# Attention score tiles below the diagonal read back from their mirror tiles, MLP and attention steps alternating

## The chip, the cores and the metric

One core of one Trainium2 chip runs the whole program in one launch. The metric is device time in microseconds of that core, from runs of the same program on the same inputs; lower is better.

## What is computed

Three layers follow each other on 24576 tokens (8 sequences of 3072) of width 256:

```python
# attention, per sequence: u, v are 3072 x 256, z is 3072 x 64
scores = matmul(z, z.T) / 3072
x = u * matmul(maximum(scores, 0) ** 2, v)
# MLP: w_in 256 x 2048, w_out 2048 x 256
h = x @ w_in
x = (h * sigmoid(h)) @ w_out
# eight experts, one per token (argmax of x @ w_gate), 256 -> 1024 -> 256
h = maximum(x[mask] @ w1[e], 0)
out[mask] = gate[mask] * output_gate[mask, e] * (h @ w2[e])
```

The score matrix of a sequence is z times its own transpose, so it is symmetric: the score of query s and key t is that of query t and key s.

## The kernel before

**Numbers.** The matmuls run on fp32r operands. To keep fp32 accuracy each operand is split into a high part (`hi`, rounded to fp32r) and the rest (`lo` = value - `hi`), and a product is three matmuls: high by high, high by low, low by high.

**Blocks and steps.** Tokens are cut into 48 blocks of 512 (`NBLK`), 6 per sequence: block (b, q) is query block q of sequence b. Attention of a block has 24 steps (`KT`), one for each key tile of 128 keys. A step has a front and a back. The front (`att_items`, lines 203 to 228) makes a score tile of 128 keys by 512 queries in PSUM with two matmuls (lines 214 and 215; z has only 64 columns, so its high and low parts are stacked on the 128 partitions of `hl`), ScalarE takes Relu (line 217) and Square (line 219) into a buffer `t1`, then `hi` is cast (line 225, VectorE; line 223, ScalarE, in some early steps), and `lo` is a VectorE subtraction (line 227), which is issued at the next step. The back (lines 230 to 247) adds the tile's product with v to the accumulator: six matmuls of 512 columns (lines 240 to 242).

The MLP of a block has 16 steps (`NF1`) of 128 hidden columns: six matmuls in front (line 271), Sigmoid on ScalarE (line 273), product on VectorE (line 275), `hi` on ScalarE (line 278), `lo` on VectorE (line 280), and twelve matmuls of 256 columns in the back (lines 305 to 307). After attention of a block `finish` (line 253, two VectorE instructions) multiplies by u, and `split_x` (lines 195 and 197) makes the MLP's operands `xh` and `xl`.

**Order.** All steps stand in one list, `items`. The main loop (lines 836 to 849) issues at index i the tasks that are due, the front of step i, the `lo` of the step before, the back of step i-3 (`LOOK`), and then further tasks as long as a credit lasts that the finished step's budget fills up. From block 3 on, the list is: 7 attention steps of block n (`PRE`), all 16 MLP steps of block n-1, the other 17 attention steps of block n. Engines run their own instructions in this order, and semaphores come from the buffers: `ps` (PSUM, 4), `acc` (2), `t0` (2), `t1` (3), `hi` and `lo` (4 each), shared by attention and MLP steps.

**Tasks.** Loads of z and v go through SP's DMA queue into a ring of four staging buffers (`raw`, `DEPTH`) in the order of a list `stream`; each use of one (`f_prep`) stages the next. Line 163 loads z, line 180 v, line 209 u (two tiles of 256 KB per block, at step 4). Per sequence there are 6 key operands `hl` and 12 pairs `vh`, `vl` to be prepared, per block one `hh`, `ll`. Routing of a finished MLP block is 16 tasks of two VectorE dot products each (`dot`, line 315), a task `pick`, a task `rank` and four indirect DMAs to the scratch tensor `scr`. The experts (from about 4320 us) read gathered rows of `scr`; there, `m2_block` (line 527) already loads 512 x 32 blocks as 128-byte pieces, eight DMAs for two tiles, and `m2_trans` (line 581) turns them with VectorE's 32x32 transpose.

Of the kernel before, what the change touches and what calls it, by code (L numbers as in the profile page):

```python
# [9 lines left out]
F32 = mybir.dt.float32  # L10
# [31 lines left out]
def moe_chain(tc, zT, uT, vp, win, wout, w12, wgT, wogT, out):  # L42
# [19 lines left out]
    NBM = min(NB, (N - NA * TQ) // TB + E // 2)  # L62
    assert NBLK > 3 and KT > 2 * PRE and NF1 >= 16 and NA <= P and NB <= P and N // P <= 256
    ZS = 2.0 ** -10
    AS = (1.0 / (S * ZS)) ** 2

    with ExitStack() as ctx:
# [117 lines left out]
        def split_x(b, q, last=False):  # L185
# [10 lines left out]
            for c in range(ND):  # L196
                nc.vector.tensor_tensor(out=l[c], in0=x[c], in1=r32(h[c]), op=ALU.subtract)

        def att_items(b, q, hold):
            st = {}  # L200
            early = (b, q) < (0, 2)

            def front(k):
                def f():
                    if k == LOOK + 1:
                        st["u"] = []
                        for c in range(ND):
                            ut = mk(ap_, [P, TQ], F32, "u", 2)
                            nc.sync.dma_start(out=ut, in_=uT[b, q, :, c, :])
                            st["u"].append(ut)  # L210
                    h, l = qs[(b, q)]
                    ps = psum()
                    lhs = hl[k // NS][:, (k % NS) * P:(k % NS + 1) * P]
                    nc.tensor.matmul(ps, lhs, h, start=True, stop=False)  # L214
                    nc.tensor.matmul(ps, lhs, l, start=False, stop=True)  # L215
                    r = mk(cp, [P, TQ], F32, "t0", 2)
                    nc.scalar.activation(r, ps, AF.Relu)  # L217
                    a = mk(cp, [P, TQ], F32, "t1", 3)
                    nc.scalar.activation(a, r, AF.Square)  # L219
                    hi = mk(cp, [P, TQ], F32R, "hi", 4)  # L220
                    lo = mk(cp, [P, TQ], F32R, "lo", 4)
                    if early and q and k % 2:
                        nc.scalar.activation(hi, a, AF.Copy)
                    else:
                        nc.vector.tensor_copy(hi, a)  # L225
                    st[k] = (hi, lo)
                    return lambda: nc.vector.tensor_tensor(out=lo, in0=a, in1=r32(hi), op=ALU.subtract)  # L227
                return f

            def back(k):  # L230
                def f():
                    hi, lo = st.pop(k)
                    if k == 0:
                        st["acc"] = accum()
                    acc = st["acc"]
                    for c in range(ND):
                        o = k % 2 * D + c * P
                        h = vh[k // 2][:, o:o + P]
                        l = vl[k // 2][:, o:o + P]
                        nc.tensor.matmul(acc[:, c, :], h, hi, start=k == 0, stop=False)  # L240
                        nc.tensor.matmul(acc[:, c, :], h, lo, start=False, stop=False)  # L241
                        nc.tensor.matmul(acc[:, c, :], l, hi, start=False, stop=k == KT - 1)  # L242
                    if k == KT - 1:
                        later(2, 1.2, finish, 0)
# [9 lines left out]

            return [Item(front(k), back(k), EARLY if early else 0.7 if q == NQ - 1 else 0.5) for k in range(KT)]

# [194 lines left out]
        def final_tables():  # L451
# [19 lines left out]
            for e in range(E):  # L471
                later(4 + 2 * e, 0.0, pad(fr, e))

# [169 lines left out]
        order = [("a", 0, 0, KT), ("a", 1, 0, KT), ("a", 2, 0, PRE), ("m", 0, 0, NF1), ("a", 2, PRE, 2 * PRE), ("m", 1, 0, NF1), ("a", 2, 2 * PRE, KT)]  # L643
        for n in range(3, NBLK):
            end = NF1 - (PRE if n == NBLK - 1 else 0)
            order += [("a", n, 0, PRE), ("m", n - 1, 0, end), ("a", n, PRE, KT), ("m", n - 1, end, NF1)]
        order += [("m", NBLK - 1, 0, NF1)]
# [23 lines left out]

        def prep(due, rel, load, use):
            stream.append((due, rel, len(stream), load, use))

# [11 lines left out]
        for n, (b, q) in enumerate(blocks):  # L686
            if q == 0:
                for j in range(NHL):
                    rel = att_step(n - 1, (j + 1) * NS - 1) + 1 if n else 0
                    prep(max(att_step(n, j * NS) - (0 if n else 2), rel), rel, load_zz(b, j), f_hl(j))  # L690
            prep(att_step(n, 0), att_step(n - 1, KT // 2) if n else 0, load_zz(b, q), f_hh((b, q)))
            if q == 0:
                for j in range(KT // 2):
                    rel = att_step(n - 1, 2 * j + 1) + LOOK + 1 if n else 0
                    due = att_step(n, 2 * j) + (0 if n else 1)
# [4 lines left out]
        def stage():  # L700
            if len(staged) < len(stream):
                t = mk(ap_, [P, TQ], F32, "raw", DEPTH)
# [3 lines left out]
        def f_prep(k):  # L706
            def f():
                while len(staged) <= k:
                    stage()
                stream[k][4](staged[k])  # L710
                if len(staged) < k + 1 + DEPTH:
                    stage()
            return f
# [3 lines left out]
        r_ = 0  # L717
        for k, (due, rel, _, _, use) in enumerate(stream):
            r_ = max(r_, rel)
# [204 lines left out]
```

## Time and profile before

| | |
|---|---|
| median of 3 runs | 5449.75 us (5448.02 to 5459.81) |
| profiled execution | 5460.9 us, its span on the engines 5459.0 us |
| TensorE (PE) busy | 5405.5 us, 99% |
| VectorE (DVE) busy | 3919.9 us, 72% |
| ScalarE (ACT) busy | 3222.5 us, 59% |
| GpSimd (POOL) busy | 476.0 us, 9% |
| DMA | 328.79 MB, mean 60 GB/s |

The span runs from the first to the last instruction of the profiled execution. Busy times of an engine are unions of its instructions' records; records of neighbouring instructions overlap, so that the distance of two starts, not the length of a record, is what an instruction takes of its engine's time. PEld is TensorE's weight load, which runs beside the matmuls; SPq is the queue that issues DMAs.

### The profile page before, as it was taken

The page shows a single profiled execution, that of the slowest core. Times are in us where ns is not written, and L with a number is a line of the kernel's source. Part 1 is how long each engine was busy: PE and PEld are TensorE (multiplying, and loading weights), DVE is VectorE, ACT ScalarE, POOL GpSimd, SP SyncE. Part 2 cuts the span into 40 slices and gives each one's busy share as a digit, 9 for nine tenths or more (in the row PEclk, how much of TensorE's full clock was granted, in tenths as well). Part 3 has the DMA queues.
Part 4 walks back from the last instruction along what each step waited for, and adds up shares of the span by engine and source line. Part 5 has one row for each costly group of instructions (what it writes and reads, how often), then busy time and mean ns, then how long its engine had stood idle before and what let it go on. Part 6 is the DMA issues. An engine that isn't in the chain of part 4 may idle for free.

```text
span 5459.0 us, 87672 instructions
## 1 busy us (share of the span) xinstructions
PE 5405.5 (99%) x30962; PEld 4717.1 (86%) x30962; DVE 3919.9 (72%) x10207; ACT 3222.5 (59%) x5692; POOL 476.0 (9%) x503
## 2 busy tenths in 40 slices
PE   7999999999999999999999999999999999999999
PEld 5888888888888888888888888888888898999999
DVE  8877776777677767767776777677677776666687
ACT  6556565665566566656665565556565555555576
POOL 3100000000000000000000000000000021111111
PEclk9999999999999999999999999999999999999999
DMA  3100100010011001000100010001000456555564
GB/s 103 35 19 24 42 17 15 28 38 16 17 31 35 16 16 49 17 19 17 50 17 15 17 50 15 17 22 44 17 9 17 124 170 195 170 178 175 166 228 161
DMA packets 279456, 328.79 MB, mean 60 GB/s; under 512 B 177502, under 2 KB 210911, under 8 KB 263265
## 3 DMA queue, kind: packets, MB, share of 16 engines
q1 hardware_dynamic: 260192, 271.20, 16.4%
q0 software_dynamic: 18816, 51.93, 2.6%
q8 instruction: 244, 4.00, 0.3%
q14 instruction: 204, 1.66, 0.1%
HBM read 268.63 MB, written 55.46 MB: 59 GB/s over the span
## 4 chain that ended last, share of the span: by engine, by line
PE 96%; DVE 2%; DMA 1%; ACT 1%; issue 0%; SPq 0%; POOL 0%; POOLq 0%; DVEq 0%; ACTq 0%
PE ps L271 19%; PE ps L604 10%; PE acc L305 10%; PE acc L306 10%; PE acc L307 10%; PE acc L242 9%; PE acc L240 9%; PE acc L241 9%; PE ps L215 5%; PE ps L214 5%; DVE lo L227 1%; DVE wg L752 0%; DVE hi L225 0%; PE ps L585 0%; DMA xg<-scr 0%
## 5 line engine op out<-in xcount | busy, mean ns | idle before, releaser
L275 DVE TENSOR_TENSOR t<-ps,t 128x512 f32<-128x512 f32 x768 | 529.8, 690 | 695.9 <-ACT t L273 694.7
L306 PE MATMUL acc<-woutl,hi 128*128 128x256 f32 x3600 | 1001.3, 278 | 0.0
L217 ACT ACTIVATE t<-ps 128x512 f32<-128x512 f32 x1152 | 685.9, 595 | 488.3 <-PE ps L215 483.6
L241 PE MATMUL acc<-lo,vh 128*128 128x512 f32 x2304 | 903.7, 392 | 26.9 <-DVE lo L227 26.6
L242 PE MATMUL acc<-hi,vl 128*128 128x512 f32 x2304 | 912.4, 396 | 0.0
L240 PE MATMUL acc<-hi,vh 128*128 128x512 f32 x2304 | 909.0, 395 | 0.0
L278 ACT ACTIVATE hi<-t 128x512 fp32r<-128x512 f32 x768 | 486.0, 633 | 666.6 <-DVE t L275 666.6
L305 PE MATMUL acc<-wouth,hi 128*128 128x256 f32 x3072 | 857.1, 279 | 0.0
L307 PE MATMUL acc<-wouth,lo 128*128 128x256 f32 x3072 | 852.6, 278 | 2.7 <-DVE lo L280 2.7
L225 DVE CAST hi<-t 128x512 fp32r<-128x512 f32 x1140 | 492.7, 432 | 462.0 <-ACT t L219 400.9
L227 DVE TENSOR_TENSOR lo<-t,hi 128x512 fp32r<-128x512 f32 x1152 | 801.4, 696 | 0.0
L219 ACT ACTIVATE t<-t 128x512 f32<-128x512 f32 x1152 | 728.2, 632 | 39.1 <-DVE lo L227 1.4
L273 ACT ACTIVATE t<-ps 128x512 f32<-128x512 f32 x768 | 457.8, 596 | 485.8 <-PE ps L271 485.6
L306 PEld LDWEIGHTS acc<-woutl,hi 128*128 128x128 f32 x3600 | 678.6, 188 | 37.5
L305 PEld LDWEIGHTS acc<-wouth,hi 128*128 128x128 f32 x3072 | 576.7, 188 | 32.1
L271 PE MATMUL ps<-xl,winh 128*128 128x512 f32 x1504 | 592.1, 394 | 0.0
L271 PE MATMUL ps<-xh,winl 128*128 128x512 f32 x1504 | 589.6, 392 | 0.0
L271 PE MATMUL ps<-xh,winh 128*128 128x512 f32 x1504 | 589.3, 392 | 0.0
L315 DVE CUSTOM_DVE_ANT_0 junk<-rec,wg 128x256 f32<-128x256 f32 x1536 | 583.7, 417 | 0.0
L307 PEld LDWEIGHTS acc<-wouth,lo 128*128 128x128 f32 x3072 | 577.7, 188 | 3.3 <-DVE lo L280 3.3
L241 PEld LDWEIGHTS acc<-lo,vh 128*128 128x128 f32 x2304 | 434.8, 189 | 144.6 <-DVE lo L227 38.7
L381 POOL DMA_INDIRECT scr<-rec,si x192 | 194.5, 1013 | 3873.1 <-ACT t L273 2853.6
(442 smaller groups left out, 9711.2 us busy)
## 6 DMA issues: line engine op xcount, KB each, us to landing
raw<-in_w_dram SPq DMA_DIRECT2D x122, 1024.0 KB, 5.9
raw<-in_zT_dram SPq DMA_DIRECT2D x192, 128.0 KB, 2.7
raw<-in_vp_dram SPq DMA_DIRECT2D x96, 256.0 KB, 2.8
u<-in_uT_dram SPq DMA_DIRECT2D x96, 256.0 KB, 2.7
xg<-scr SPq DMA_DIRECT2D x39, 544.0 KB
x<-scr SPq DMA_DIRECT2D x304, 64.0 KB, 2.2
wo<-in_wogT_dram SPq DMA_DIRECT2D x61, 128.0 KB, 7.8
xg<-scr SPq DMA_DIRECT2D x22, 272.0 KB
```

The lines of the kernel that those rows point to most:

```text
L217: nc.scalar.activation(r, ps, AF.Relu)
L219: nc.scalar.activation(a, r, AF.Square)
L227: return lambda: nc.vector.tensor_tensor(out=lo, in0=a, in1=r32(hi), op=ALU.subtract)
L240: nc.tensor.matmul(acc[:, c, :], h, hi, start=k == 0, stop=False)
L241: nc.tensor.matmul(acc[:, c, :], h, lo, start=False, stop=False)
L242: nc.tensor.matmul(acc[:, c, :], l, hi, start=False, stop=k == KT - 1)
L271: nc.tensor.matmul(ps, win_at(w, c, f_), x[c], start=c == 0 and i == 0, stop=c == ND - 1 and i == 2)
L305: nc.tensor.matmul(y[:, s, :], a, wh, start=first and s % per_bank == 0, stop=False, skip_group_check=True)
L306: nc.tensor.matmul(y[:, s, :], a, wl, start=False, stop=False, skip_group_check=True)
L307: nc.tensor.matmul(y[:, s, :], l, wh, start=False, stop=last, skip_group_check=True)
L315: nc.vector.tensor_tensor_reduce(out=j, in0=a, in1=w, scale=1.0, scalar=0.0, op0=ALU.mult, op1=ALU.add, accum_out=res)
L604: nc.tensor.matmul(ps[:, 0:T], w[:, o:o + P], y[c][:, 0:T], start=c == 0 and j == 0, stop=c == ND - 1 and j == 2)
```

## The change

For a tile (block q, key tile k) whose keys lie in an earlier query block (k // 4 < q; in sequence 0 only for q of 3 and more) the front no longer computes the score. Its values stand, transposed, in the four tiles that block k // 4 computed for the keys of block q. Those are written to DRAM when they are made (`keep`, 256 KB each, into a 512 x 512 tensor `sym`). `load_sym` reads a 512 x 128 part of it with four DMAs of 128-byte pieces into a staging buffer, so that each 32 x 32 block is in its place but not turned; `flip` turns the blocks with a VectorE transpose into `t1`; ScalarE copies `hi` from it, VectorE subtracts `lo`, and the back is as before. A block with mirrored tiles takes its key tiles in another order (`key_order`): first the four with the next block's keys, whose mirrors that block will read, or in a sequence's last block the four on the diagonal; then the others. A load is not staged before its mirror tiles have been issued (`since`).

Besides, from block 3 on one MLP step of block n-1 and one attention step of block n alternate after the first 7 attention steps; the cast to `hi` moves to ScalarE in all later blocks except the even steps of query block 0; budgets for tasks change (`spare`); release times of `hl` and `v` follow the new key order; each use stages up to two loads; and the padding tasks of the expert tables stand 8 steps apart instead of 2.

```diff
--- before.py
+++ after.py
@@ -60,7 +60,7 @@
     NA = max(0, (NSNAP * TQ - E * (TQ - 1) + TQ - 1) // TQ)
     NB = (N - NA * TQ + E * (TB - 1)) // TB
     NBM = min(NB, (N - NA * TQ) // TB + E // 2)
-    assert NBLK > 3 and KT > 2 * PRE and NF1 >= 16 and NA <= P and NB <= P and N // P <= 256
+    assert NBLK > 3 and KT >= PRE + NF1 and KT > 2 * PRE and NF1 >= 16 and NA <= P and NB <= P and N // P <= 256
     ZS = 2.0 ** -10
     AS = (1.0 / (S * ZS)) ** 2
 
@@ -196,18 +196,68 @@
             for c in range(ND):
                 nc.vector.tensor_tensor(out=l[c], in0=x[c], in1=r32(h[c]), op=ALU.subtract)
 
+
+        def mirrored(b, q, k):
+            return k // NS < q and (b, q) >= (0, 3)
+
+        def key_order(b, q):
+            if not any(mirrored(b, q, k) for k in range(KT)):
+                return list(range(KT))
+            lead = list(range((q + 1) * NS, (q + 2) * NS)) if q < NQ - 1 else list(range(q * NS, KT))
+            return lead + [k for k in range(KT) if k not in lead]
+
+        sym, flipped = {}, {}
+
+        def load_sym(b, q, k):
+            def f(t):
+                src = sym[b, k // NS, q]
+                for g in range(P // SQ):
+                    o = k % NS * P + g * SQ
+                    nc.sync.dma_start(out=t[g * SQ:(g + 1) * SQ].rearrange("t (j d) -> t j d", d=SQ),
+                                      in_=src[:, o:o + SQ].rearrange("(j t) d -> t j d", t=SQ))
+            return f
+
+        def flip(b, q, k):
+            def f(t):
+                a = flipped[b, q, k] = mk(cp, [P, TQ], F32, "t1", 3)
+                nc.vector.transpose(a, t)
+            return f
+
+        def keep(b, q, k, a):
+            key = (b, q, k // NS)
+            if key not in sym:
+                sym[key] = dram.tile([TQ, TQ], F32, name=f"sym_{b}_{q}_{k // NS}")
+            nc.sync.dma_start(out=sym[key][k % NS * P:(k % NS + 1) * P, :], in_=a)
+
         def att_items(b, q, hold):
             st = {}
             early = (b, q) < (0, 2)
-
-            def front(k):
+            ks = key_order(b, q)
+
+            def front(i):
+                k = ks[i]
+
+                def low(a, hi, lo):
+                    def f():
+                        nc.vector.tensor_tensor(out=lo, in0=a, in1=r32(hi), op=ALU.subtract)
+                        if k // NS > q and mirrored(b, k // NS, q * NS):
+                            keep(b, q, k, a)
+                    return f
+
                 def f():
-                    if k == LOOK + 1:
+                    if i == LOOK + 1:
                         st["u"] = []
                         for c in range(ND):
                             ut = mk(ap_, [P, TQ], F32, "u", 2)
                             nc.sync.dma_start(out=ut, in_=uT[b, q, :, c, :])
                             st["u"].append(ut)
+                    hi = mk(cp, [P, TQ], F32R, "hi", 4)
+                    lo = mk(cp, [P, TQ], F32R, "lo", 4)
+                    st[i] = (hi, lo)
+                    if mirrored(b, q, k):
+                        a = flipped.pop((b, q, k))
+                        nc.scalar.activation(hi, a, AF.Copy)
+                        return low(a, hi, lo)
                     h, l = qs[(b, q)]
                     ps = psum()
                     lhs = hl[k // NS][:, (k % NS) * P:(k % NS + 1) * P]
@@ -217,30 +267,29 @@
                     nc.scalar.activation(r, ps, AF.Relu)
                     a = mk(cp, [P, TQ], F32, "t1", 3)
                     nc.scalar.activation(a, r, AF.Square)
-                    hi = mk(cp, [P, TQ], F32R, "hi", 4)
-                    lo = mk(cp, [P, TQ], F32R, "lo", 4)
-                    if early and q and k % 2:
+                    if (early and q and k % 2) or (not early and (q or k % 2)):
                         nc.scalar.activation(hi, a, AF.Copy)
                     else:
                         nc.vector.tensor_copy(hi, a)
-                    st[k] = (hi, lo)
-                    return lambda: nc.vector.tensor_tensor(out=lo, in0=a, in1=r32(hi), op=ALU.subtract)
+                    return low(a, hi, lo)
                 return f
 
-            def back(k):
+            def back(i):
+                k = ks[i]
+
                 def f():
-                    hi, lo = st.pop(k)
-                    if k == 0:
+                    hi, lo = st.pop(i)
+                    if i == 0:
                         st["acc"] = accum()
                     acc = st["acc"]
                     for c in range(ND):
                         o = k % 2 * D + c * P
                         h = vh[k // 2][:, o:o + P]
                         l = vl[k // 2][:, o:o + P]
-                        nc.tensor.matmul(acc[:, c, :], h, hi, start=k == 0, stop=False)
+                        nc.tensor.matmul(acc[:, c, :], h, hi, start=i == 0, stop=False)
                         nc.tensor.matmul(acc[:, c, :], h, lo, start=False, stop=False)
-                        nc.tensor.matmul(acc[:, c, :], l, hi, start=False, stop=k == KT - 1)
-                    if k == KT - 1:
+                        nc.tensor.matmul(acc[:, c, :], l, hi, start=False, stop=i == KT - 1)
+                    if i == KT - 1:
                         later(2, 1.2, finish, 0)
                         if hold != "held":
                             later(3, 1.2, lambda: split_x(b, q, hold == "last"), 0)
@@ -252,7 +301,10 @@
                     x.append(mk(ap_, [P, TQ], F32, "raw", DEPTH) if hold == "last" else mk(cp, [P, TQ], F32, "x", 2))
                     nc.vector.scalar_tensor_tensor(out=x[c], in0=st["acc"][:, c, :], scalar=AS, in1=st["u"][c], op0=ALU.mult, op1=ALU.mult)
 
-            return [Item(front(k), back(k), EARLY if early else 0.7 if q == NQ - 1 else 0.5) for k in range(KT)]
+            def spare(k):
+                return EARLY if early else 0.0 if mirrored(b, q, k) else 0.8
+
+            return [Item(front(i), back(i), spare(k)) for i, k in enumerate(ks)]
 
 
         recs = {}
@@ -469,7 +521,7 @@
             fr = cp.tile([P, E], I32, name="fr")
             nc.vector.tensor_tensor(out=fr, in0=n, in1=ecap, op=ALU.add)
             for e in range(E):
-                later(4 + 2 * e, 0.0, pad(fr, e))
+                later(4 + NF2 * e, 0.0, pad(fr, e))
 
         fill = cp.tile([P, TB // P, RW], F32, name="fill")
 
@@ -642,8 +694,11 @@
         blocks = [(b, q) for b in range(B) for q in range(NQ)]
         order = [("a", 0, 0, KT), ("a", 1, 0, KT), ("a", 2, 0, PRE), ("m", 0, 0, NF1), ("a", 2, PRE, 2 * PRE), ("m", 1, 0, NF1), ("a", 2, 2 * PRE, KT)]
         for n in range(3, NBLK):
+            order += [("a", n, 0, PRE)]
             end = NF1 - (PRE if n == NBLK - 1 else 0)
-            order += [("a", n, 0, PRE), ("m", n - 1, 0, end), ("a", n, PRE, KT), ("m", n - 1, end, NF1)]
+            for k in range(end):
+                order += [("m", n - 1, k, k + 1), ("a", n, PRE + k, PRE + k + 1)]
+            order += [("a", n, PRE + end, KT), ("m", n - 1, end, NF1)]
         order += [("m", NBLK - 1, 0, NF1)]
         steps = {}
         for n, bq in enumerate(blocks):
@@ -669,8 +724,12 @@
         qs = {}
         stream = []
 
-        def prep(due, rel, load, use):
-            stream.append((due, rel, len(stream), load, use))
+        def prep(due, rel, load, use, since=0):
+            stream.append((due, rel, len(stream), load, use, since))
+
+        def last_use(n, keys):
+            o = key_order(*blocks[n])
+            return max(att_step(n, o.index(k)) for k in keys)
 
         def f_hl(j):
             return lambda t: prep_hl(j, t)
@@ -686,19 +745,24 @@
         for n, (b, q) in enumerate(blocks):
             if q == 0:
                 for j in range(NHL):
-                    rel = att_step(n - 1, (j + 1) * NS - 1) + 1 if n else 0
+                    rel = last_use(n - 1, range(j * NS, (j + 1) * NS)) + 1 if n else 0
                     prep(max(att_step(n, j * NS) - (0 if n else 2), rel), rel, load_zz(b, j), f_hl(j))
             prep(att_step(n, 0), att_step(n - 1, KT // 2) if n else 0, load_zz(b, q), f_hh((b, q)))
+            for i, k in enumerate(key_order(b, q)):
+                if mirrored(b, q, k):
+                    o = key_order(b, k // NS)
+                    since = max(att_step(n - q + k // NS, o.index(q * NS + s)) for s in range(NS)) + 2
+                    prep(att_step(n, i), att_step(n, i), load_sym(b, q, k), flip(b, q, k), since)
             if q == 0:
                 for j in range(KT // 2):
-                    rel = att_step(n - 1, 2 * j + 1) + LOOK + 1 if n else 0
+                    rel = last_use(n - 1, (2 * j, 2 * j + 1)) + LOOK + 1 if n else 0
                     due = att_step(n, 2 * j) + (0 if n else 1)
                     prep(due, rel, load_flat(vp[b, :, 2 * j:2 * j + 2, :].rearrange("p a d -> p (a d)")), f_split(vh[j], vl[j], b, due))
         stream.sort()
         staged = []
 
         def stage():
-            if len(staged) < len(stream):
+            if len(staged) < len(stream) and stream[len(staged)][5] <= now[0]:
                 t = mk(ap_, [P, TQ], F32, "raw", DEPTH)
                 stream[len(staged)][3](t)
                 staged.append(t)
@@ -708,14 +772,15 @@
                 while len(staged) <= k:
                     stage()
                 stream[k][4](staged[k])
-                if len(staged) < k + 1 + DEPTH:
-                    stage()
+                for _ in range(2):
+                    if len(staged) < k + 1 + DEPTH:
+                        stage()
             return f
 
         for _ in range(DEPTH):
             stage()
         r_ = 0
-        for k, (due, rel, _, _, use) in enumerate(stream):
+        for k, (due, rel, *_) in enumerate(stream):
             r_ = max(r_, rel)
             assert r_ <= due
             task(due, r_, 0.6, f_prep(k))
```

## Rows read from the trace of the kernel before

**Rows 1.** The page: busy time of TensorE, its busy tenths and granted clock in 40 slices.
```profile
PE 5405.5 (99%) x30962; PEld 4717.1 (86%) x30962; DVE 3919.9 (72%) x10207; ACT 3222.5 (59%) x5692; POOL 476.0 (9%) x503
...
PE   7999999999999999999999999999999999999999
...
PEclk9999999999999999999999999999999999999999
```

**Rows 2.** The page: the chain that ended last, shares by engine and by line.
```profile
PE 96%; DVE 2%; DMA 1%; ACT 1%; issue 0%; SPq 0%; POOL 0%; POOLq 0%; DVEq 0%; ACTq 0%
PE ps L271 19%; PE ps L604 10%; PE acc L305 10%; PE acc L306 10%; PE acc L307 10%; PE acc L242 9%; PE acc L240 9%; PE acc L241 9%; PE ps L215 5%; PE ps L214 5%; DVE lo L227 1%; DVE wg L752 0%; DVE hi L225 0%; PE ps L585 0%; DMA xg<-scr 0%
```

**Rows 3.** Busy time by stage: stretch, its length, then per engine busy us (count).
```profile
310.00:4150.00 3840.00, 3840.00 (x20898) 3305.73 (x20898) 2727.66 (x7247) 2290.39 (x3806) 183.80 (x220) 1.00 0.08 25
...
2000.00:2710.00 710.00, 710.00 (x3861) 611.05 (x3860) 510.15 (x1352) 427.89 (x714) 33.22 (x40) 1.00 0.09 28
```

**Rows 4.** Timeline of TensorE at a block's start: start us, length us, instruction.
```profile
2043.85 0.39 PE L214 MATMUL ps<-hh,hl 128*128 128x512 f32 x1
...
2045.70 0.39 PE L214 MATMUL ps<-hh,hl 128*128 128x512 f32 x1
...
2050.11 0.39 PE L241 MATMUL acc<-lo,vh 128*128 128x512 f32 x1
...
2056.82 0.39 PE L271 MATMUL ps<-xh,winh 128*128 128x512 f32 x1
...
2058.20 0.39 PE L240 MATMUL acc<-hi,vh 128*128 128x512 f32 x1
...
2065.07 0.39 PE L271 MATMUL ps<-xh,winh 128*128 128x512 f32 x1
...
2067.82 0.39 PE L271 MATMUL ps<-xh,winh 128*128 128x512 f32 x1
```

**Rows 5.** ScalarE: timeline of the same block, and a group of line 278.
```profile
2044.52 0.60 ACT L217 ACTIVATE t<-ps 128x512 f32<-128x512 f32 x1 [0.59 <-PE ps L215]
2045.15 0.63 ACT L219 ACTIVATE t<-t 128x512 f32<-128x512 f32 x1
...
L278 ACT ACTIVATE hi<-t 128x512 fp32r<-128x512 f32 x768 | 486.0, 633 | 666.6 <-DVE t L275 666.6
```

**Rows 6.** Timeline of VectorE in the same block.
```profile
2046.15 0.68 DVE L227 TENSOR_TENSOR lo<-t,hi 128x512 fp32r<-128x512 f32 x1
...
2051.71 0.68 DVE L227 TENSOR_TENSOR lo<-t,hi 128x512 fp32r<-128x512 f32 x1
2052.32 0.42 DVE L315 CUSTOM_DVE_ANT_0 junk<-rec,wg 128x256 f32<-128x256 f32 x1
...
2053.01 1.28 DVE L253 SCALAR_TENSOR_TENSOR x<-acc,u 128x512 f32<-128x512 f32 x2
2054.21 0.41 DVE L225 CAST hi<-t 128x512 fp32r<-128x512 f32 x1
2054.54 0.68 DVE L227 TENSOR_TENSOR lo<-t,hi 128x512 fp32r<-128x512 f32 x1
```

**Rows 7.** One tile's instructions: the VectorE transpose, ns min/median/max.
```profile
L581 DVE STREAM_TRANSPOSE yT<-x x76: 694/701/714, 4317.0 to 5152.0; 128x512 f32<-128x512 f32 x76
```

**Rows 8.** Line 527's loads: issue ns, landing, eight issues, and a stretch (last: clock, DMA share, GB/s).
```profile
L527 SPq DMA_DIRECT2D x<-scr x304: 316/338/3672, 4304.6 to 5132.8; - x152
...
x<-scr SPq DMA_DIRECT2D x304, 64.0 KB, 2.2
...
4588.64 4.74 SPq L527 DMA_DIRECT2D x<-scr  x8
...
4588.00:4593.50 5.50, 5.50 (x37) 4.97 (x37) 2.50 (x4) 3.18 (x7) 0.97 (x1) 1.00 0.54 97
```

**Rows 9.** Line 209's loads of 256 KB: issue ns and landing, min/median/max.
```profile
L209 SPq DMA_DIRECT2D u<-in_uT_dram x96: 327/333/967, 18.0 to 4183.1; - x96
...
DMA to landing us min/median/max: 2.5/2.7/5.6
```

## The prediction

> **What bounds the kernel now.** I read the page first, then the chain of waits, then busy time by stage, then the timeline inside one block. The page gives TensorE 99% of the span, at the full 2.4 GHz level (granted clock 9 or more tenths in every slice) [rows 1]; the chain that ended last is 96% TensorE, and its two score lines, 214 and 215, are 5% each [rows 2]. By stage, TensorE is busy 3840.00 of 3840 us from 310 to 4150 us, and from 2000 to 2710 us, where VectorE has 510.15 of 710 us (72%) and ScalarE 427.89 (60%) [rows 3]. So in the attention and MLP stage nothing but TensorE's own stream sets the time; whatever leaves it is gained, until another engine comes late.
>
> Price of that stream: one attention step with 8 matmuls of 512 columns runs from 2043.85 to 2045.70, 1.85 us, 231 ns each; the six MLP front matmuls take 2056.82 to 2058.20, 1.38 us; a whole MLP step 2065.07 to 2067.82, 2.75 us [rows 4]. Records show 0.39 us because they overlap; the start-to-start distance is the price. A block is 24 x 1.85 + 16 x 2.75 = 88.4 us. Check: 482 matmuls per block (192 + 288 + 2 for ranks), 3861 in 710 us, so 88.6 us [rows 3].
>
> **The change, part by part.**
>
> *Score matmuls removed.* A batch has 6 query blocks; key tiles below the diagonal number 4 x (0+1+2+3+4+5) = 60. Batches 1 to 7 give 420; batch 0 only blocks 3 to 5, 4 x 12 = 48. 468 tiles x 2 matmuls x 0.231 us = 216 us off the path. A mirrored step then costs TensorE 1.39 us.
>
> *Vector and scalar work.* A mirrored step loses Relu and Square (0.63 us from one start to the next [rows 5]) and gains one ScalarE copy (0.63 us like line 278 [rows 5]) and one VectorE transpose. The nearest row, line 581, same shape, has 694/701/714 ns [rows 7]; other 512-wide VectorE instructions start about 0.08 us before the one ahead has ended in its record, so 0.62 us. The cast of `hi` (0.34 us) leaves VectorE in all later blocks but for half the steps of query block 0; `lo` stays, 0.60 us [rows 6]. Per block, worst VectorE case (q=5, 20 mirrored): 63.8 us now, - 24 x 0.34 + 20 x 0.62 = 68 us, against TensorE 88.6 - 20 x 0.46 = 79.4 us. Worst ScalarE case (q=1): 53.5 + 20 x 0.63 - 4 x 0.63 = 63.6 against 86.8 us. On the average neither becomes the bound.
>
> *Loads.* Each mirrored tile is read by four DMAs of 64 KB in 128-byte pieces. The trace has just this form in line 527: issue 338 ns in the median, eight of them issued in 4.74 us, landing 2.2 us after issue [rows 8]. So 2.4 us of SP's queue per tile. DMA share then is 0.54 [rows 8], little. The tightest stretch is q=5, where mirrored and MLP steps alternate: a tile is wanted every 1.39 + 2.75 = 4.14 us. SP is 57% used, and four staged slots are four tiles, 16 us, ahead. Hidden. In the runs of consecutive mirrored steps (4, 5, 6) the tiles were staged in the block before. If that cover were gone, a tile would cost 2.4 + 2.2 us in the open.
>
> Here the Trainium skill speaks against the change: "DMA: Bandwidth & Descriptors", section "Rules for kernel authors", calls a transposing copy by a plain DMA with a rearranged access pattern 19 times slower than the hardware transpose. Taking the 2.7 us landing of a plain 256 KB load [rows 9] as one unit, an estimate by that page is 51 us per tile, and 468 x 51 us = 24 ms. The trace does not bear it out: here whole 128-byte rows are moved and the 32x32 turn is VectorE's, and two tiles' worth were issued in 4.74 us. It gets no more than 1 in 100, inside rival three.
>
> *Writes.* 468 mirrored tiles need 468 writes of 256 KB (`keep`), one issue each on SP, which waits for Square. The trace has no such write; the bounds are nothing and, by the nearest 256 KB row, u's load, 2.7 us to landing, at most 5.6 [rows 9]. New is that `t1`, a ring of three, is now held until the write has landed. Three attention steps later is 5.5 us, so 0.33 + 2.7 fits; costed at nothing, kept for rival two.
>
> *Order.* Alternating MLP and attention steps changes no count. But the seven attention steps (PRE) that open a block stay together, and there the slack shrinks. Today `lo` of step 0 has ended at 2046.83 and is wanted at 2050.11: 3.3 us ahead [rows 4, 6]. With mirrored steps 4 to 6, TensorE comes for step 3 after 3 x 1.39 instead of 3 x 1.85 us, 1.4 us earlier, and ScalarE's copy instead of VectorE's cast makes `lo` 0.3 us later. In the same steps VectorE has `finish` (1.20 us [rows 6]) and the split of x (1.2 us), both just when now, plus transposes, plus two routing dots a task (0.69 us [rows 6]), which the credit lets in from step 3 on (MLP now ends two steps before the block does, plus LOOK+2).
>
> Time from the first matmul of step 0. ScalarE (step 0's Relu at 0.67 [rows 4, 5], 1.86 us per step with the copy, two copies of the MLP record in between) ends `hi` of step 2 at 7.0 and of step 3 at 8.8. VectorE in order: lo(2) to 7.6, two dot tasks to 9.0, transpose 4 to 9.6, finish to 10.8, lo(3) to 11.45. TensorE starts step 6 at 4 x 1.85 + 2 x 1.39 = 10.2 and wants lo(3) at 10.4: 1.05 us stall, ending 12.6. VectorE: dots to 12.1, transpose 5 to 12.7, split to 13.3 and 13.9, lo(4) to 14.5. The MLP front wants xl at 13.1: 0.25 us. Then dots 15.2, transpose 6 15.8, lo(5) 16.5, wanted at 15.9: 0.6 us. After that each alternating pair asks VectorE for 0.62 + 0.60 + 0.61 + 0.60 + some 1.05 of dots = 3.5 of 4.14 us, and it catches up. Sum 1.9 us per block, in 38 blocks with mirrored tiles: 72 us. Bounds: nothing (if VectorE is 2 us earlier than that) and 3 us. The value taken is the walk's.
>
> At the seven batch changes the 19 preparations (`hl`, `hh`, `v`) can no longer run in the block before, since their release is made later than the last mirrored tile's. Seven fall in steps 0 to 6, ScalarE 7 x 0.6 = 4 us on top of some 12 of 13 us. With 3 us of slack I take 1.5 us each, 10 us; bounds 0 and 4.
>
> *Sum.* 5460.9 - 216 + 72 + 10 = 5327 us for the profiled execution. It lies 11 us above the median of the runs, 5449.75, so 5316 us there.
>
> **Rivals.** One: VectorE is never late, all 216 us are kept: 5450 - 216 = 5234 us. For it: 28% of VectorE is free and the three steps of lookahead cover 4 us. Against: the walk above.
>
> Two: the ring of `t1` decides. At step 4 `keep` of step 3 is queued on SP behind four block loads (2.4 us) and u's two, and transpose 6 needs that buffer: landing at about 15.3, wanted at 15.2, by a hair. If writes land at 5.6 instead of 2.7 us [rows 9], VectorE stands 2.9 us in each of the 30 blocks that both keep and mirror: 87 us more, 5403 us.
>
> Three, the other sign: the block loads become the bound in q=5 and q=4. Line 527's source rows lie 1088 bytes apart, the new ones 2048. From 5.2 us per tile on (20 x 5.2 = 104 against 79.4 us, 16 x 5.2 = 83 against 81.2; 8 blocks each: 211 us) the gain is gone; at three times 2.4, 7.1 us, it is 20 x 7.1 - 79.4 = 63, 16 x 7.1 - 81.2 = 32 and 12 x 7.1 - 83.1 = 2 us, 8 x 97 = 776 us, some 6010 us. Against: 2.4 us is issue, not transfer, and share 0.54. The Trainium skill, the same page, section "Latency and other measured facts", has copies falling to half their rate at row pitches that are large powers of two, from 512 KiB up; the half would be 4.7 us per tile and, as an estimate, 5450 - 216 + 8 x 14.6 = 5350 us. No run here shows a 2048-byte pitch of 128-byte pieces.
>
> **How the numbers follow.** Forecast (1 to 3 us per block, 5272 to 5368 us) 0.50; rival one (up to 1 us) 0.27; rival two 0.08; rival three 0.10; the rest, unforeseen, 0.05, of it 0.03 within 0.2%, which is about what a measurement here can tell. So faster 0.85, same 0.03, slower 0.12. The range 5230 to 5400 holds rivals one and most of two, 0.85 in all.
>
> **What would show it.** Score matmuls 1368 instead of 2304. TensorE waiting for `lo` of steps 3 and 5 and for `xl`, once in each block with mirrored tiles, some 70 us by the waits; block distance 79.4 to 88.6 us plus that. Transposes at 0.70 us, loads landing near 2.2 us with no wait of VectorE for them. Wrong if VectorE waits for DMAs (rivals two, three), or if TensorE is still 100% busy (rival one).

## The result and the profile after

The changed kernel takes 5387.2 us (median of 4 runs, 5382.7 to 5387.9), before 5449.87 us; the ratio is 0.988, 95% interval 0.9862 to 0.9897. So it is 63 us faster, where 134 us were forecast. Its profiled execution spans 5385.1 us.

The page of the changed kernel: busy time, and the chain that ended last by engine [rows 1, 2].
```profile
PE 5237.8 (97%) x30026; PEld 4536.8 (84%) x30026; DVE 3830.7 (71%) x9655; ACT 3233.8 (60%) x5776; POOL 483.3 (9%) x503
...
PE 80%; DVE 9%; ACT 5%; DMA 3%; issue 2%; SPq 0%; DVEq 0%; ACTq 0%; POOL 0%; POOLq 0%
```
TensorE has 936 matmuls fewer (468 tiles, two each), but is no longer full: VectorE, ScalarE and DMA have 17% of the chain, 4% before. The stage from block 3 on, by windows [rows 3], has TensorE idle for 97 us:
```profile
279.00:4080.00 3801.00, 3704.05 (x20030) 3148.50 (x20029) 2653.24 (x6750) 2305.07 (x3890) 184.72 (x215) 1.00 0.36 85
```
What it waited for there (us in total, times, longest), from 279 to 4250 us:
```profile
PE acc L290 <- DVE lo L242: 57.8, 83, 1.2
PE ps L264 <- ACT hh L174: 13.5, 5, 3.0
PE ps L264 <- DVE hl L169: 13.1, 7, 1.9
PE acc L359 <- DVE lo L332: 8.3, 16, 0.9
PE ps L264 <- DVE vl L93: 4.8, 2, 2.4
PE ps L265 <- DVE ll L175: 1.3, 6, 0.2
```
The first row is mostly the block starts of the forecast; the waits for `hh`, `hl`, `vl` and `ll` are those of the seven sequence changes, and those of line 359 (MLP) lie in the block after them.

**A block start.** Timeline of VectorE and, below, of TensorE in a block with mirrored tiles [rows 4, 6]. Line 242 is `lo`, 367 the dots, 223 the transpose, 302 `finish`, 290 the matmul that needs `lo`.
```profile
1151.41 0.69 DVE L242 TENSOR_TENSOR lo<-t,hi 128x512 fp32r<-128x512 f32 x1 [1.61 <-ACT hi L271]
1152.02 0.42 DVE L367 CUSTOM_DVE_ANT_0 junk<-rec,wg 128x256 f32<-128x256 f32 x1
...
1153.40 0.70 DVE L223 STREAM_TRANSPOSE t<-raw 128x512 f32<-128x512 f32 x1
1154.03 1.25 DVE L302 SCALAR_TENSOR_TENSOR x<-acc,u 128x512 f32<-128x512 f32 x2
1155.21 0.67 DVE L242 TENSOR_TENSOR lo<-t,hi 128x512 fp32r<-128x512 f32 x1
```
```profile
1154.32 0.39 PE L289 MATMUL acc<-hi,vh 128*128 128x512 f32 x1
1155.93 0.50 PE L290 MATMUL acc<-lo,vh 128*128 128x512 f32 x1 [1.23 <-DVE lo L242]
1156.27 0.40 PE L291 MATMUL acc<-hi,vl 128*128 128x512 f32 x1
...
1157.42 0.40 PE L323 MATMUL ps<-xh,winl 128*128 128x512 f32 x1
1157.82 0.50 PE L323 MATMUL ps<-xl,winh 128*128 128x512 f32 x1
1158.16 0.39 PE L323 MATMUL ps<-xh,winh 128*128 128x512 f32 x1
...
1160.28 0.40 PE L289 MATMUL acc<-hi,vh 128*128 128x512 f32 x1
1160.91 0.50 PE L290 MATMUL acc<-lo,vh 128*128 128x512 f32 x1 [0.23 <-DVE lo L242]
1161.25 0.39 PE L291 MATMUL acc<-hi,vl 128*128 128x512 f32 x1
```
VectorE's order is that of the forecast: lo(2), four dots, transpose, `finish`, lo(3), where lo(k) is `lo` of step k. Over the 0.23 us that a matmul takes, TensorE loses 1.38 us at lo(3), 0.17 at xl, 0.40 at lo(5): 1.95 us, forecast 1.05 + 0.25 + 0.6 = 1.9. The matmul behind each of these three starts 0.34 us later instead of 0.23; with that the block loses 2.3 us.

**A sequence change.** First SP, ScalarE and TensorE at step 0, then ScalarE, VectorE and TensorE at step 4 of the same block.
```profile
2096.41 0.47 SPq L163 DMA_DIRECT2D raw<-in_zT_dram  x1
...
2098.23 0.61 ACT L168 ACTIVATE hl<-raw 128x512 fp32r<-128x512 f32 x1
2098.75 0.61 ACT L95 ACTIVATE vh<-raw 128x512 fp32r<-128x512 f32 x1
2099.70 0.63 ACT L174 ACTIVATE hh<-raw 128x512 fp32r<-128x512 f32 x1 [0.34 <-DMA raw<-in_zT_dram]
...
2097.48 0.40 PE L291 MATMUL acc<-hi,vl 128*128 128x512 f32 x1
2100.38 0.53 PE L264 MATMUL ps<-hh,hl 128*128 128x512 f32 x1 [2.50 <-ACT hh L174]
2101.11 0.80 PE L265 MATMUL ps<-ll,hl 128*128 128x512 f32 x1 [0.19 <-DVE ll L175]
2101.70 0.41 PE L357 MATMUL acc<-wouth,hi 128*128 128x256 f32 x1
2101.91 0.41 PE L358 MATMUL acc<-woutl,hi 128*128 128x256 f32 x1
...
2109.86 0.63 ACT L271 ACTIVATE hi<-t 128x512 fp32r<-128x512 f32 x1
2110.40 0.61 ACT L168 ACTIVATE hl<-raw 128x512 fp32r<-128x512 f32 x1
...
2111.04 0.69 DVE L169 TENSOR_TENSOR hl<-raw,hl 64x512 fp32r<-64x512 f32 x1 [0.87 <-ACT hl L168]
...
2111.79 0.50 PE L264 MATMUL ps<-hh,hl 128*128 128x512 f32 x1 [1.87 <-DVE hl L169]
```
The load of `hh` is issued at 2096.41, when the transpose of a mirrored tile has freed a staging buffer. ScalarE takes `hl` and `vh` first, and then stands 0.34 us until that load has landed; it starts `hh` at 2099.70, and TensorE stands 2.5 us. The chain that ended last there goes through the load, not through ScalarE's order (from the critical chain of 2095 to 2102 us):
```profile
2095.76 0.63 DVE t L223
...
2096.93 2.69 DMA raw<-in_zT_dram
...
2099.70 0.64 ACT hh L174
```
At all seven changes ScalarE waits for this load, 0.25 to 0.86 us. Had it landed sooner, `hh` would still have come behind `vh`, here 0.34 us earlier: load and order end close together. Four steps later the next `hl` stands in ScalarE's order behind the copy of step 3, and TensorE stands 1.9 us. In between, the 256-column matmuls start 0.21 us apart instead of some 0.115: after the idle stretch the granted clock was 0.55, mostly the lower of its two levels, which costs 1.7 us in 3.8 (stretch, length, per engine busy us, then clock, DMA share and GB/s):
```profile
2097.90:2100.30 2.40, 0.00 (x0) 0.00 (x0) 1.63 (x3) 2.06 (x4) 0.00 (x0) 1.00 0.68 189
2100.30:2104.10 3.80, 3.52 (x14) 3.08 (x15) 1.56 (x3) 2.16 (x5) 0.00 (x0) 0.55 0.71 204
```

**Loads and writes.** Line 223, the transpose, and what it waited for; then line 216, the issues of the block loads, four to a tile (ns min/median/max) [rows 7, 8].
```profile
L223 DVE STREAM_TRANSPOSE t<-raw x468: 699/704/715, 278.5 to 4187.2; 128x512 f32<-128x512 f32 x156
...
  DMA raw<-sym: 1.4, 1
...
L216 SPq DMA_DIRECT2D raw<-sym x1872: 302/487/2066, 99.9 to 4184.3; - x188
```
VectorE waits for a block load once in the whole run, 1.4 us.

### The profile page after: what moved, and what is told of

Read it like the earlier page. It is cut to its first block, busy times and chain, and to the rows that moved or that the text cites. A ratio compares the mean times of both kernels' runs of the same rounds, so it can differ in the third digit from the quotient of the medians.

```text
span 5385.1 us, 88728 instructions
## 1 busy us (share of the span) xinstructions
PE 5237.8 (97%) x30026; PEld 4536.8 (84%) x30026; DVE 3830.7 (71%) x9655; ACT 3233.8 (60%) x5776; POOL 483.3 (9%) x503
## 4 chain that ended last, share of the span: by engine, by line
PE 80%; DVE 9%; ACT 5%; DMA 3%; issue 2%; SPq 0%; DVEq 0%; ACTq 0%; POOL 0%; POOLq 0%
PE ps L323 17%; PE ps L656 10%; PE acc L357 10%; PE acc L359 10%; PE acc L358 10%; PE acc L290 7%; PE acc L291 6%; PE acc L289 6%; DVE lo L242 2%; PE ps L265 2%; PE ps L264 2%; ACT t L269 2%; DVE junk L367 1%; DVE t L223 1%; ACT t L267 1%
## 5 line engine op out<-in xcount | busy, mean ns | idle before, releaser
L290 PE MATMUL acc<-lo,vh 128*128 128x512 f32 x2304 | 922.5, 400 | 82.8 <-DVE lo L242 82.6
L242 DVE TENSOR_TENSOR lo<-t,hi 128x512 fp32r<-128x512 f32 x1152 | 796.8, 693 | 249.9 <-ACT hi L271 249.9
L330 ACT ACTIVATE hi<-t 128x512 fp32r<-128x512 f32 x768 | 486.0, 633 | 661.8 <-DVE t L327 647.4
L325 ACT ACTIVATE t<-ps 128x512 f32<-128x512 f32 x768 | 456.7, 595 | 452.3 <-PE ps L323 450.1
L367 DVE CUSTOM_DVE_ANT_0 junk<-rec,wg 128x256 f32<-128x256 f32 x1536 | 570.3, 419 | 0.0
L259 ACT ACTIVATE hi<-t 128x512 fp32r<-128x512 f32 x468 | 296.1, 633 | 427.0 <-DVE t L223 333.3
L332 DVE TENSOR_TENSOR lo<-t,hi 128x512 fp32r<-128x512 f32 x768 | 518.9, 676 | 24.5
L289 PEld LDWEIGHTS acc<-hi,vh 128*128 128x128 f32 x2304 | 435.8, 189 | 98.0
```

The lines of the kernel that those rows point to most:

```text
L289: nc.tensor.matmul(acc[:, c, :], h, hi, start=i == 0, stop=False)
L332: return lambda: nc.vector.tensor_tensor(out=lo, in0=g, in1=r32(hi), op=ALU.subtract)
L367: nc.vector.tensor_tensor_reduce(out=j, in0=a, in1=w, scale=1.0, scalar=0.0, op0=ALU.mult, op1=ALU.add, accum_out=res)
```

## The experiments

Times are medians where a range is given, else one run. Each is set against 5387 us of the changed kernel; before took 5445 to 5449 us beside them (medians). Executions of one kernel differ by up to 16 us (before: 5444 to 5460), so a smaller difference between single runs shows little by itself.

**Preparations earlier.** `prep` takes a shift (`early`), which is 16 steps for `hl`, `hh` and `v` of a new sequence and 0 for all else (the three calls that pass it are not shown):
```diff
-        def prep(due, rel, load, use, since=0):
+        def prep(due, rel, load, use, since=0, early=0):
+            due = max(due - early, rel)
             stream.append((due, rel, len(stream), load, use, since))
```


> One edit: the preparations of hl, hh and v for a new sequence get due times 16 steps earlier (not before their own release), so in the ordered list they no longer stand behind the last mirrored tiles. Theory A (pinned preparations): at each of the 7 sequence changes TensorE loses about 10.4 us in the changed kernel (first front waits for hh, step 4 waits for hl, the clock falls once, MLP steps wait for lo after that); with the preparations spread over the block before, 1 us is left of it: 5387 - 65 = 5322 us, within 15. Rival B: VectorE and ScalarE in query block 5 have no room for ten more preparations (6 us each on VectorE), so the loss only moves ahead: 5375 to 5400 us.

5370 us: in neither range, closer to B. TensorE no longer waits for `hh` and `hl` at the changes, but longer for `lo`, in the second half of query block 5 and at the start of the block after it. Its waits over the whole run (line 291 here is line 290 of the changed kernel, with 82.6 us there):
```profile
PE acc L291 <- DVE lo L243: 97.2, 120, 3.1
PE acc L360 <- DVE lo L333: 18.9, 18, 1.5
PE ps L265 <- ACT hh L175: 6.0, 1, 6.0
```
The one wait for `hh` lies at the start of the run. Taking the pin away is not enough; the bunch of preparations moves.

**Dots later.**
```diff
-            rel = moe_end[n] + LOOK + 2
+            rel = moe_end[n] + LOOK + 2 + (5 if 2 <= n < NBLK - 2 else 0)
```


> One edit: the routing tasks of a block are released 5 steps later, so that no dot product stands in VectorE's queue in steps 3 to 7 of the next attention block. Theory A: the waits for lo of step 3, for xl and for lo of step 5, together 2.3 us in each of 38 blocks, come from VectorE's order (dots, then transpose, finish and split, before these lo); they vanish: 5387 - 85 = 5302 us, within 15. Rival C: the wait comes from t1, held by the writes to DRAM (the transpose of step 6 waits for the write of step 3), or from ScalarE's longer chain: no more than 15 us are won, 5372 us or more.

5321 us. The wait for line 242 is gone but for 2.9 us from 290 to 4200 us (57.8 in the changed kernel); there is one new wait of 24 us, at 4152 us, for an MLP step's `lo` (two windows of TensorE's waits):
```profile
PE acc L290 <- DVE lo L242: 2.9, 7, 0.9
...
PE acc L359 <- DVE lo L332: 24.0, 1, 24.0
```
That is 4 us outside the range of theory A; without that one wait it is 5297 us, inside it, and not rival C (the writes).

**Both.**

> Both edits of the two kernels before. Theory A: what is left is TensorE's own stream, 5450 - 216 = 5234 us, and some 1 us per sequence change and small rests: 5235 to 5260 us. Rivals B and C: 5360 us or more. If VectorE, with 15% of its time free in query block 5, becomes late elsewhere once both waits are gone, the time lies between, 5270 to 5340 us.

5316 us (5310.9 to 5325.2; ratio 0.9761, 0.9745 to 0.9777), with the same wait of 24 us. Between the theories: earlier preparations add next to nothing to later dots (5 us).

**No preparations.** Leaves out the preparations of `hl` and `v` from the second sequence on; first beside the later dots (not in the last 4 blocks, which avoids the wait of 24 us), then alone:
```diff
-                    prep(max(att_step(n, j * NS) - (0 if n else 2), rel), rel, load_zz(b, j), f_hl(j))
+                    if not n:
+                        prep(max(att_step(n, j * NS) - (0 if n else 2), rel), rel, load_zz(b, j), f_hl(j))
```
(the same for `v`)

> Leaves out the preparations of hl and v for the second and later sequences (their attention uses the first sequence's operands); the routing tasks are released 5 steps later as in the second kernel, but not for the last 4 blocks, where that release cost one wait of 24 us. Theory A: with the preparations gone and the dots out of the way nothing else holds TensorE in the blocks from 3 on, so the sum of the two is the whole loss: 5450 - 216 = 5234 us plus small rests, 5235 to 5255 us. Rival F: part of the loss is VectorE or the block loads in query block 5 itself: 5270 us or more.

> The changed kernel; left out are the preparations of hl and v for the second and later sequences (their attention uses the first sequence's operands), nothing else. Theory A: 7 x 9 us, the whole loss at the sequence changes but for 1.5 us that hh costs there: 5387 - 62 = 5325 us, within 10; the 2.3 us in each of 38 blocks stay. Rival: the loss there comes from the block itself, 5360 us or more.

5236 us and 5328 us. These two part the loss: 5387 - 5328 = 59 us for the preparations, 5328 - 5236 = 92 us for the dots in VectorE's order, and 5236 is about the floor of rival one (5234). TensorE is all but full again in the first of them, idle for 13.6 us, mostly for `hh`, which is still prepared there (windows):
```profile
279.00:4060.00 3781.00, 3767.41 (x20738) 3247.03 (x20737) 2675.70 (x6881) 2303.89 (x3875) 192.83 (x225) 1.00 0.34 79
```
Between the changed kernel and the one that leaves out the preparations alone, TensorE's waits from 279 to 4250 us fall from 98.8 to 64.3 us, and ten stretches at the lower clock like the one shown, some 1.7 us each, are gone: 34 and 17 of the 59 us. The rest was not parted.

**Preparations spread.** All preparations are made again: `hl` 0 to 3 in query block 4 of the sequence before, `hh` and seven `v` one by one over block 5, dots later except in the last 4 blocks (not shown: the due time of `hh`, step 23 of block 5):
```diff
+                    if n and j < 4:
+                        rel = att_step(n - 2, 0)
+                        due = att_step(n - 2, 8 + 3 * j)
...
+                    if n and j < 7:
+                        due = att_step(n - 1, 0) + (14, 17, 20, 26, 30, 34, 38)[j]
```


> Four staging buffers, dots 5 steps later (not in the last 4 blocks); four of the six hl of a new sequence are prepared in query block 4 before, three attention steps apart, hh and seven of the twelve v one by one over query block 5. Theory G: loads that don't come in bunches are issued in time; some 2 us are left per sequence change: 5234 + 14 + small rests, 5245 to 5265 us. Rival B (VectorE is full in query block 5): 5285 to 5300 us.

5258 us (5257.9 to 5266.3), ratio to before 0.9651 (0.9635 to 0.9667): the fastest that computes everything, 22 us above the kernel without preparations. Its waits from 279 to 4010 us:
```profile
PE acc L290 <- DVE lo L242: 11.5, 11, 2.1
PE acc L359 <- DVE lo L332: 8.5, 7, 1.4
PE acc L289 <- ACT rec L349: 5.2, 7, 0.8
```
Moving the due times of `hh` and `v` a few steps did not better it:

> The seventh kernel with the due times of hh and v a few steps earlier (the last at step 37 of 40 of query block 5) and the later release of dots for one more block. The two waits left in the seventh kernel at the sequence change (1.4 us for lo of the last MLP step, 0.9 us for the copy of the MLP's sums on ScalarE) come from the v prepared at step 38; they shrink: 5245 to 5257 us. If VectorE is simply full there: 5256 to 5262 us.

5265 us (5264.0 to 5267.3), above both ranges.

**A longer ring of staging buffers** (`DEPTH` 4 to 5). With bunched preparations, first with one scratch tile for the dots, then with three of half the size; and with spread ones:

> The third kernel (preparations 16 steps earlier, dots 5 steps later, there 5316 us, of which 24 us are one wait near the end that is mended here) with five staging buffers instead of four; the room comes from a scratch tile. Theory G: what was left in query block 5 and at the sequence change (some 8 us of 7 times) comes from loads that are issued when a staging buffer comes free, less than their landing time ahead, with ScalarE standing before hl until they land; a fifth buffer issues each load one use earlier: 5292 - 35 = 5257 us, within 15. Rival B: VectorE has no room there: 5285 to 5300 us.

> The sixth kernel again (preparations 16 steps earlier in bunches, dots later, five staging buffers) with three scratch tiles. Theory I (bunches of preparations stand in ScalarE's and VectorE's order; the loads matter little): 5270 to 5290 us. Theory G: 5257 us or less.

> The seventh kernel (spaced preparations, later dots) with five staging buffers, scratch tiles in a 2-byte type. Theory I: in the seventh kernel what is left at the sequence changes is the order of ScalarE's and VectorE's work, not the loads: 5255 to 5262 us. Theory G (loads issued too late): 5240 to 5250 us.

5289, 5284 and 5263 us (5262.3 to 5267.1): against 5316 - 24 = 5292 us the ring is worth 3 to 8 us beside bunches, which single runs cannot tell from nothing, and nothing beside spread preparations. Theory G falls for preparations that have been moved; there the order of ScalarE's and VectorE's work is what is left. A longer ring in the changed kernel itself, where the load of `hh` ends the first wait, was not run.

**A longer ring of t1** (3 to 4), again with one scratch tile and then with three:

> The changed kernel with four t1 buffers instead of three (room from the junk tile). Theory A: t1, held by the writes to DRAM, is waited for 15 times in all (ScalarE's Square and VectorE's product, 29 us, all near the sequence changes), and these waits lie beside the preparations, so 0 to 15 us are won: 5372 to 5388 us, and the waits at steps 3 and 5 of a block stay. Rival two of the prediction (t1 decides in the 30 blocks that keep and mirror): 5330 us or less.

> The changed kernel with four t1 buffers; the room comes from scratch tiles in a 2-byte type, so the dots keep three of them. Theory A: 2.3 us per block stay, only the waits for t1 near the sequence changes go: 5372 to 5388 us. Rival two of the prediction (writes to DRAM hold t1): 5330 us or less.

5398 and 5371 us. With one scratch tile two dots no longer start 0.35 but 0.46 us apart, and TensorE's waits for line 242 grow from 82.6 to 102.0 us in the whole run, as they should where it waits for VectorE's order:
```profile
1243.72 0.42 DVE L367 CUSTOM_DVE_ANT_0 junk<-rec,wg 128x256 f32<-128x256 f32 x1
...
1244.18 0.42 DVE L367 CUSTOM_DVE_ANT_0 junk<-rec,wg 128x256 f32<-128x256 f32 x1
```
With three, 16 us are won; TensorE's waits for line 242 stay, 83.0 us in the whole run against 82.6, so it is not the block starts that gain. From 279 to 4250 us its waits for `lo` in the MLP (line 359) fall from 8.3 to 0.8 us; the other 8 us were not traced.

**No alternation**, the old order of steps:

> The changed kernel with the old order of steps (7 attention steps, all MLP steps, 17 attention steps); mirrored tiles as in the change. Theory A: in the 17 consecutive attention steps a tile is wanted every 1.39 us, but SP needs 2.4 us to issue its four loads; beyond the four staged tiles each costs 1.0 us: 13 tiles in query block 5, 9, 5 and 1 in blocks 4, 3 and 2, 28 us per sequence, 225 us in all: 5610 us, with VectorE waiting for DMAs in these steps. Rival D (loads are cheaper than their issue, and VectorE with 1.22 us per mirrored step keeps up): 5370 to 5410 us.

5592 us. VectorE waits for block loads (its waits), and SP issues 36 of them, nine tiles, in 20.40 us, 2.27 us per tile (SP's timeline):
```profile
DVE t L223 <- DMA raw<-sym: 159.0, 175, 2.3
...
2073.98 20.40 SPq L216 DMA_DIRECT2D raw<-sym  x36
```

**Plain loads**, one DMA per tile of 128 rows as they stand; this leaves out the rearranging, so the values are others (the body of the loop, four DMAs of 32 partitions in 128-byte pieces, is not shown):
```diff
-                for g in range(P // SQ):
...
+                nc.sync.dma_start(out=t, in_=src[k % NS * P:(k % NS + 1) * P, :])
```


> The changed kernel with each mirrored tile loaded by one plain DMA of 256 KB (2 KB rows) instead of four with 128-byte pieces; the values are then not the mirror tile's. Theory A: the block loads are hidden (VectorE waits for them once, 1.4 us, in the whole run), so at most the loads at the sequence changes come a little earlier: 5375 to 5390 us. Rival three of the prediction (the small pieces hold up staging or share the DMA engines with the other loads): 5360 us or less.

5390 us, within the range of theory A: the loads are hidden.

**Alternation alone** (`mirrored` false for every tile):

> The change without mirrored tiles (every score is computed; new order of steps, casts on ScalarE, budgets and release times stay). Theory A: 216 us of TensorE's stream come back and the preparations are no longer pinned behind mirrored tiles, so TensorE is full again: the time before, 5440 to 5460 us. Rival H: the new order itself makes VectorE or ScalarE late at block starts: 5480 us or more.

5432 us, 16 us faster than before beside it; neither was expected. In its trace most blocks follow each other 88.3 instead of 88.7 us apart, and the time behind the last attention matmul is 1192 us, as in the changed kernel, instead of 1209 (the profiled execution of before is one of its longer ones). The padding tasks (below) have some 5 us of that; why the rest is shorter is open. So some of the 63 us may not come from the mirrored tiles: this one run lies 11 us below the fastest of before.

**Padding tasks** 2 steps apart again:

> The changed kernel with the padding tasks 2 steps apart as before the change. If that edit made the expert stage shorter (1153 us in the trace of before, 1135 in that of the changed kernel), it gets longer again: 5393 to 5405 us, with a wait of TensorE in the expert stage. If not (the stage differs from run to run, or by another cause): 5380 to 5390 us.

5390 us. A wait of TensorE in the expert stage is back that the changed kernel has not, and in the trace the time behind the last attention matmul is 1197 us against 1192; the time of the whole run does not tell it from the changed kernel's:
```profile
PE acc L357 <- ACT hi L659: 3.4, 1, 3.4
```

## Why the prediction was off

- *Bound.* Right: TensorE's own stream was all. 936 matmuls at 0.231 us are 216 us, and with the two waits out of the way the time is 5236 us, forecast as the floor 5234. That they meet to 2 us is in part chance: alternation alone took 5432 us in its one run, and 216 less is 5216; the kernel at 5236 still has 13.6 us of waits in the stage from block 3 on.
- *Vector and scalar work, loads.* Right: transposes 704 ns (701 forecast), 2.27 us of SP per tile in the run without alternation (2.4), loads hidden as long as the steps alternate, and without alternation 205 us lost where 223 were worked out. The 2048-byte pitch here shows no loss (2.27 us of issue per tile, 2.4 at 1088 bytes): rival three did not come. The row on pitches in the Trainium skill ("DMA: Bandwidth & Descriptors", "Latency and other measured facts") begins at 512 KiB, with 207 GB/s where 214 are the full rate, and comes to half at 4 MiB; it says nothing of 2048 bytes.
- *Order, block starts.* Mechanism and places right. The walk's sum was met to a tenth in the block shown (1.95 us for 1.9), but its terms were not (1.38, 0.17 and 0.40 us for 1.05, 0.25 and 0.6), so that was luck in part, and it left out that the matmul behind each wait is late too. In time the order of the dots cost 92 us in 38 blocks, 2.4 us each, forecast 72; the 2.3 us of the block shown would make 87.
- *Sequence changes.* This is the step that failed: "With 3 us of slack I take 1.5 us each, 10 us; bounds 0 and 4." Leaving these preparations out gives 59 us back, 8.4 us per change, and the two bounds did not hold it. The cause was named (releases later than the last mirrored tile's), but the price was taken from sums of ScalarE's time against slack. What it left out: the load of `hh` is issued only when a mirrored tile frees a staging buffer, and lands when TensorE already stands (2.5 us); a preparation due at the step that uses it stands in ScalarE's order behind the step before (1.9 us); TensorE's clock is mostly at its lower level after the first wait (17 us in all ten such stretches); and the MLP steps that follow wait for `lo` (8.3 us in all).
- *Rivals.* One was the floor, but for the waits above. Two, the ring of `t1`, is worth 16 us in one run, but not at the block starts, where it had been put; at the sequence changes the prediction had costed it at nothing.
- *Sum.* 216 - 92 - 59 - 2 (5236 against 5234) = 63 us. This closes because the last three terms are the differences between 5387, 5328, 5236 and 5234; the forecast had 216 - 72 - 10. The upper end of its range, 5368, is not the sum of its own bounds, 5450 - 216 + 38 x 3 + 7 x 4 = 5376 us.

## What to carry to other kernels

Where an engine is full, taking work from it is worth the whole only if every engine behind it keeps its slack: go through each place where order is fixed (block starts, changes of operands), write down for each queue what stands ahead of the awaited instruction, when its load can be issued, and price it there; VectorE's average of 71% did not show the 92 us. A list that is served in order passes one entry's release on to all behind it, so adding entries with exact due times pins the others, and spreading those over earlier steps was worth more here than more buffers. The dots and the spread preparations took two short edits and brought the gain from 63 to 186 us.

## What was not expected of the hardware

A scratch tile that is only written and never read still paces VectorE: with one instead of three, dot products started 0.46 instead of 0.35 us apart. A wait of TensorE of 2.5 us was followed by 3.8 us at a granted clock of 0.55, so that this wait cost 1.7 us more than its length.
